# ScalarE in written order through sixteen attention pairs, with the next tile's split, the late exp and the shared values product at new places

## The chip, the cores and the metric

The kernel runs on one core of a Trainium2 chip. The metric is the device time of one execution in microseconds (us), as a median of several. The engines are TensorE (PE, matmuls), VectorE (DVE), ScalarE (ACT), GpSimd (POOL) and SyncE (SP), which issues most DMAs. Each engine runs its own instructions in order; between engines semaphores make an instruction wait for another's result.

## What is computed

```python
scores = cap * np.tanh(scale * np.matmul(q, k.transpose(0, 1, 3, 2)) / cap)   # 4 x 12 heads, 448 x 64
attn = np.exp(scores - max); attn /= attn.sum(-1) + 1e-9
x = np.matmul(attn, v)                     # -> 1792 tokens x 768
h = x @ w_in                               # 768 -> 1024
solu = h * softmax(h)
ln = (solu - mean) / np.sqrt(var + 1e-6) * g_ln
x = ln @ w_out                             # 1024 -> 768
logits = x @ w_gate + modality_bias[modality_id]
e_idx = np.argmax(logits, axis=1)          # one of 8 experts for each token
out[mask] = gate_w * (np.maximum(x[mask] @ w1[e], 0) @ w2[e])
```

## The kernel before

Three stages share one program. **Attention** goes over 24 pairs (b, p): batch b of 4, two heads of 64 in a pair p of 6. The first eight pairs are *plain*, in the code's word, and run while weights are loaded and split (0 to 94 us). The sixteen *late* pairs (n = 8 to 23, that is (1,2) to (3,5)) run from 94 to some 368 us, interleaved with the first **SoLU tiles** t of 128 tokens (14 in all; the rest runs until 460 us). Then come routing and **eight experts** (460 to 728 us).

A late pair has 448 keys: three chunks of 128 and 64 left over. The left-over keys of an even p and of p + 1 share one tile: chunk "h", whose scores, tanh and exp (e_h) are made in the second half of the even pair, and whose product with the values, q, is made for both pairs at once by `a_quarters`. Names in rows carry b, p and chunk: sc1_5_0 are the scores of pair (1,5), chunk 0; e their tanh and then exp; es sums of e; av the product of e with the values; X the attention result of a batch; kh, kl, qh, ql the high and low parts of k and q, cast by ACT or DVE (for q of pairs 11, 15 and 23, that is (1,5), (2,3) and (3,5), by ACT). rt and rb (three for a batch) bring the reciprocal sums of the batch before, by which X is multiplied.

A tile of the SoLU part has these steps: `m_split` splits X into xh and xl, `m_h` multiplies (h, 36 matmuls of 512 columns, three products of high and low parts), `m_act` takes the row maximum, exp (u), h times u and the statistics of the LayerNorm, `m_tr` transposes u on PE (lt) and splits it into lh and ll, `m_y` multiplies by w_out (y, two halves), and `m_out` scales y (ys), takes one small exp for the router (junk) and stores it. lg are the router's logits, computed by DVE from y, and read by junk.

`unit(n, cp)` writes one half of a pair: scores and tanh (`a_scp`), exp (`a_exp`), some SoLU steps (`fill`), products with the values (`a_av`), parts of the finish of the batch before (`finish`), sums (`a_esp`), and the split of the next pair (`a_split`). SoLU steps wait in the list `msteps`; `fill` takes as many as a rate allows, and `settle` takes more where the written clock says that no PSUM tile is free.

The order in which an engine runs is that of the code where a `manual_schedule` names the engine, and is otherwise chosen by the framework's scheduler. Through the late pairs only PE is named: ACT, DVE, POOL and SP are placed by the scheduler. PSUM holds three large tiles "A" (128 x 2 x 512) that go round among sc, h, lt, y, q, sum, rt and rb, in the order in which the program asks for them. So the first matmul into one waits until the last reader of its previous content, on ACT or DVE, is done.

Of the kernel before, what the change touches and what calls it, by code (L numbers as in the profile page):

```python
# [41 lines left out]
EARLY = 10  # L42
# [37 lines left out]
XCD = (1, 2, 3, 4, 5, 7, 9, 10, 12, 13, 14, 15, 16, 17, 18, 19, 20)  # L80
VACT = 0
OGA = 5
W = (0.6, 0.8, 0.45)
FW = (1, 0.7, 1.3)

# [2 lines left out]
def attn_moe_kernel(ctx, tc, kq, vv, vl, w_in, w_out, packed, ids, mbias, w1, w2, out):  # L88
# [543 lines left out]
    def m_act(t):  # L632
        s = st[t]
        h = s.pop("h")
        clock.leave(f"h{t}", 4.6)
        clock.ready[t] = clock.t + 7.2
        clock.work(1.1)
        u = mp.tile([P, 2, 512], F32, tag="m4", name=f"u{t}", bufs=4)
        sm = mp.tile([P, 8], F32, tag="sm", name=f"sm{t}", bufs=4)
        s["sm"] = sm  # L640
        dve.tensor_reduce(sm[:, 0:1], h, axis=AX.XY, op=ALU.max, negate=True)
        act.activation(u, h, AF.Exp, bias=sm[:, 0:1], accum_out=sm[:, 1:2])
        dve.tensor_mul(u, u, h)
        bn = mp.tile([P, 2, 6], F32, tag="bn", name=f"bn{t}")
        for i in range(2):
            dve.bn_stats(bn[:, i, :], u[:, i, :])
        dve.bn_aggr(sm[:, 2:4], bn)
        dve.tensor_scalar(u, u, sm[:, 2:3], None, op0=ALU.subtract)
        s["u"] = u
        (dve if t in SMD else pool).tensor_scalar(sm[:, 1:2], sm[:, 1:2], 1e-9, None, op0=ALU.add)  # L650
        dve.reciprocal(sm[:, 4:5], sm[:, 1:2])
        pool.tensor_tensor(out=sm[:, 5:6], in0=sm[:, 4:5], in1=sm[:, 4:5], op=ALU.mult)
        pool.tensor_tensor(out=sm[:, 5:6], in0=sm[:, 5:6], in1=sm[:, 3:4], op=ALU.mult)
        pool.tensor_scalar(sm[:, 5:6], sm[:, 5:6], 1e-6, None, op0=ALU.add)
        pool.tensor_tensor(out=sm[:, 6:7], in0=sm[:, 5:6], in1=mhalf, op=ALU.pow)
        pool.tensor_tensor(out=sm[:, 7:8], in0=sm[:, 6:7], in1=sm[:, 4:5], op=ALU.mult)
# [167 lines left out]
    def a_av(b, p, chunks=range(4)):  # L824

        if 0 in chunks:
            avt[b, p] = btile(f"av{b}_{p}")
            if p == 0:
                spt[b] = psS.tile([P, 512], F32, tag="S", name=f"S{b}")
        o, v = avt[b, p], vt[b, p]  # L830
        end = 3 if plain(b, p) else 2
        clock.spend(0.75 * len(chunks), "columns")
        if direct(b, p) or p % 2 and end in chunks:
            clock.spend(0.75, "strips")
        for c in chunks:
            for j in range(2):
                pe.matmul(o[64 * j:64 * j + 64, :S], v[:, c, 64 * j:64 * j + 64], et[b, p, c][:, j, :],  # L837
                          start=(c == 0), stop=(c == end))
        if direct(b, p):
            for c in chunks:  # L840
                for j in range(2):
                    g = 2 * j + c % 2
                    pe.matmul(spt[b][32 * g:32 * g + 32, :S], zone[:CK, 31 - p:63 - p], et[b, p, c][:, j, :],
                              start=(p == 0 and c < 2), stop=(p == NP - 1 and c > 1))
        elif p % 2 and end in chunks:
            for j in range(2):
                for i in range(2):
                    g, pp = 2 * j + i, p - 1 + i
                    pe.matmul(spt[b][32 * g:32 * g + 32, :S], zone[:, 31 - pp:63 - pp], est[b, pp][:, j, :],
                              start=(p == 1), stop=(p == NP - 1))  # L850
        if end in chunks:
            x = xtile(b)[:, p, :]
            if convs and b + p:
                later["x"].append(lambda: dve.tensor_copy(x, o[:, :S]))
            elif plain(b, p):
                (dve.tensor_copy if b * NP + p in XCD else act.copy)(x, o[:, :S])
            else:
                dve.tensor_add(x, x, o[:, :S])
            if p == NP - 1:
                a_ssb(b)  # L860

    def a_quarters(b, p):
        settle()
        t = atile(f"q{b}_{p}")
        for g in range(2):
            r = slice(64 * g, 64 * g + 64)
            for j in range(2):
                c = slice(64 * j, 64 * j + 64)
                pe.matmul(t[c, g, :S], vt[b, p][r, 3, c], et[b, p, "h"][r, j, :], start=True, stop=True)
        clock.spend(0.75, "quarters")  # L870
        clock.work(1.0)
        clock.leave(f"q{b}_{p}", clock.act - clock.t + 0.1)
        act.copy(xtile(b)[:, p:p + 2, :], t[:, :, :S])

    sums = {}

# [46 lines left out]
    msteps, drained = [], set()  # L923

    def push_tile(t):
        msteps.append((0.0, lambda: m_split(t), 0))
        hs = [(W[0], lambda hf=hf, d=d: m_h(t, hf, d), hf == 0 and d == 0) for hf in range(2) for d in range(ND)]
        if t and t - 1 not in drained:
            hs.insert(ND + (TRP[t - NTILE + 3] if t > NTILE - 4 else 0), (W[1], lambda: m_tr(t - 1), 1, t - 1))
        msteps.extend(hs)  # L930
        msteps.append((0.0, lambda: m_act(t), 0))
        final = t == NTILE - 1
        if final:
            msteps.append((0.0, lambda: e_first(), 0))
        if t and t - 1 not in drained:
            push_y(t - 1, t if final and TRO else None)
        if final:
            if not TRO:
                msteps.append((0.9, lambda: m_tr(t), 1))
            n = len(msteps)  # L940
            push_y(t)
            msteps.insert(n + ETD, (0.0, lambda: e_tr(), 1))
# [13 lines left out]

    def pick():

        if len(msteps[0]) > 3 and clock.t < clock.ready.get(msteps[0][3], 0.0):
            return int(all(x[0] == W[0] and not x[2] for x in msteps[1:4]))  # L960
        return 0

# [38 lines left out]
    def unit(n, cp):  # L1001
        nonlocal mp
        b, p = pairs[n]
        early = plain(b, p) and b > 0
        strips, trs = later["strip"], later["pe"]
        later["strip"], later["pe"] = [], []

        def run(fs):
            while fs:
                fs.pop(0)()  # L1010

        late_ = not plain(b, p)
        if late_ and not cp:
            m = pairs[n - 1]
            if plain(*m):
                a_av(*m, chunks=(2, 3))
            else:
                if not m[1] % 2:
                    a_quarters(*m)
                a_av(*m, chunks=(2,))  # L1020
        a_scp(b, p, cp)
        if n == 1 and not cp:
            a_av(*pairs[0], chunks=(2, 3))
        flush("cast")
        if early and p:
            flush("gate")
            if not cp:
                finish(b - 1, 4)
            else:
                run(strips)  # L1030
                flush("gate")
                cv.release()
                mp = tc.alloc_tile_pool(name="mp", bufs=2, reuse_waits="tile")
                do_step()
        a_exp(b, p, cp)
        if early and cp and not p:
            flush("gate", "sub")
            finish(b - 1, 2)
        if late_:
            pass  # L1040
        elif cp == 0 and n > 1:
            a_av(*pairs[n - 1], chunks=(2, 3))
        elif cp:
            a_av(b, p, chunks=(0, 1))
        if convs:
            convs.pop(0)()
        flush("gate", "x")
        run(strips)
        flush("gate")
        if early and p and not cp:  # L1050
            finish(b - 1, 5)
        run(trs)
        if early and cp and not p:
            flush("gate")
            finish(b - 1, 3)
        fill(FW[0])
        if late_ and cp:
            a_av(b, p, chunks=(0, 1))
        if b > 0 and not plain(b, p):
            finish(b - 1, 4 * p + 2 * cp)  # L1060
        flush("sub")
        if n == 1 and cp:
            setup_third(*tables)
        a_esp(b, p, cp)
        if n + 1 < len(pairs):
            a_split(*pairs[n + 1], cp)
        fill(FW[1])
        if cp == 1 and n + 2 < len(pairs):
            a_load(*pairs[n + 2])
        if cp == 0 and n + 1 < len(pairs):  # L1070
            v_load(*pairs[n + 1])
        fill(FW[2])
        if b > 0 and not plain(b, p):
            finish(b - 1, 4 * p + 2 * cp + 1)
        while early and p and sums_:
            conv_og(sums_[0], atile(f"po{sums_.pop()}")[:, 0, :NE])
# [3 lines left out]
    with tc.manual_schedule(engines={ET.PE, ET.Activation, ET.DVE, ET.SP}):  # L1080
# [17 lines left out]
        for n in range(FIXED):  # L1098
            unit(n, 0)
            unit(n, 1)  # L1100
    with tc.manual_schedule(engines={ET.PE}):
        for n in range(FIXED, len(pairs)):
            unit(n, 0)
            unit(n, 1)
# [697 lines left out]
```

## Time and profile before

| | us |
|---|---|
| median of 3 runs (730.03 to 731.84) | 731.14 |
| the profiled execution | 729.99 |
| its span, first to last instruction | 728.3 |
| PE busy | 711.6 (98% of the span) |
| DVE busy | 433.4 (60%) |
| ACT busy | 372.3 (51%) |
| POOL busy | 112.6 (15%) |

The profiled execution is 1.7 us longer than its span. The chain of work that ended last is to 87% on PE, to 4% each on DVE and ACT. Busy time of PE comes from modelled ends of pipelined matmuls, so neighbouring rows overlap a little. A row of the timeline gives start, duration, engine, line, operation, output <- input, partitions x elements, how many instructions it groups, and in brackets the engine's idle time ahead of it and what ended it.

### The profile page before, as it was taken

The page shows a single profiled execution, that of the slowest core. Times are in us where ns is not written, and L with a number is a line of the kernel's source. Part 1 is how long each engine was busy: PE and PEld are TensorE (multiplying, and loading weights), DVE is VectorE, ACT ScalarE, POOL GpSimd, SP SyncE. Part 2 cuts the span into 40 slices and gives each one's busy share as a digit, 9 for nine tenths or more (in the row PEclk, how much of TensorE's full clock was granted, in tenths as well). Part 3 has the DMA queues.
Part 4 walks back from the last instruction along what each step waited for, and adds up shares of the span by engine and source line. Part 5 has one row for each costly group of instructions (what it writes and reads, how often), then busy time and mean ns, then how long its engine had stood idle before and what let it go on. Part 6 is the DMA issues. An engine that isn't in the chain of part 4 may idle for free.

```text
span 728.3 us, 11174 instructions
## 1 busy us (share of the span) xinstructions
PE 711.6 (98%) x4294; PEld 544.2 (75%) x4294; DVE 433.4 (60%) x726; ACT 372.3 (51%) x506; POOL 112.6 (15%) x208
## 2 busy tenths in 40 slices
PE   8999999999999999999999999999999999999996
PEld 3344456475667666677698999998879998799995
DVE  7999656666656648455466546965256173473632
ACT  7999666665556554555521225354154162553522
POOL 5000111311012021121041211114010220002011
PEclk9999999999999999999999999999999999999998
DMA  7776120211111120200003101579928359574550
GB/s 253 262 269 241 41 76 12 88 62 38 61 41 60 46 75 13 84 15 34 22 23 124 44 30 59 172 283 320 408 76 279 120 173 402 236 238 152 210 167 26
DMA packets 29569, 97.14 MB, mean 133 GB/s; under 512 B 4087, under 2 KB 6149, under 8 KB 28738
## 3 DMA queue, kind: packets, MB, share of 16 engines
q1 hardware_dynamic: 25794, 79.47, 30.7%
q0 software_dynamic: 3568, 16.83, 6.4%
q8 instruction: 36, 0.59, 0.3%
q14 instruction: 27, 0.22, 0.1%
q10 hardware_dynamic: 144, 0.03, 0.1%
HBM read 85.24 MB, written 11.27 MB: 133 GB/s over the span
## 4 chain that ended last, share of the span: by engine, by line
PE 87%; DVE 4%; ACT 4%; DMA 2%; issue 2%; POOLq 1%; POOL 0%; SPq 0%; another core or an unknown queue 0%; DVEq 0%
PE av L837 7%; PE sc L790 7%; PE y L683 6%; PE h L627 6%; PE y L686 5%; PE y L684 5%; PE h L630 5%; PE h L628 5%; PE poD L1506 3%; PE poD L1508 3%; PE poD L1507 3%; PE phD L1400 3%; PE phD L1402 3%; PE phD L1401 3%; DMA rawc<-in_w_out_dram 2%
## 5 line engine op out<-in xcount | busy, mean ns | idle before, releaser
L797 ACT ACTIVATE e<-sc,sc 128x896 f32<-128x896 f32 (+1 forms) x80 | 78.6, 1004 | 58.6 <-PE sc L790 58.4
L803 ACT ACTIVATE e<-e,pk 128x896 f32<-128x896 f32 (+1 forms) x80 | 81.8, 1045 | 1.3
L683 PE MATMUL y<-wouh,lh 128*128 128x392 f32 (+1 forms) x224 | 78.8, 352 | 1.1 <-ACT e L797 1.1
L684 PE MATMUL y<-woul,lh 128*128 128x392 f32 (+1 forms) x224 | 75.8, 339 | 0.0
L837 PE MATMUL av<-e,v 128*64 128x448 f32 (+1 forms) x320 | 70.9, 555 | 0.7 <-ACT e L803 0.7
L686 PE MATMUL y<-wouh,ll 128*128 128x392 f32 (+1 forms) x224 | 71.3, 339 | 0.0
L627 PE MATMUL h<-winh,xh 128*128 128x512 f32 x168 | 69.6, 414 | 0.4 <-ACT xh L610 0.4
L628 PE MATMUL h<-winl,xh 128*128 128x512 f32 x168 | 66.0, 393 | 0.0
L630 PE MATMUL h<-winh,xl 128*128 128x512 f32 x168 | 61.2, 391 | 0.0
L683 PEld LDWEIGHTS y<-wouh,lh 128*128 128x128 f32 x224 | 42.0, 188 | 12.9 <-issue 10.3
L837 PEld LDWEIGHTS av<-e,v 128*64 128x64 f32 (+1 forms) x320 | 18.6, 135 | 39.3 <-issue 25.9
L1344 DVE TENSOR_TENSOR wl_D<-raw_D,wh_D 128x768 fp32r<-128x768 f32 (+1 forms) x28 | 29.9, 1071 | 27.0 <-ACT wh_D L1343 26.7
L627 PEld LDWEIGHTS h<-winh,xh 128*128 128x128 f32 x168 | 31.5, 188 | 18.0 <-issue 11.2
L1344 DVE TENSOR_TENSOR wl_H<-raw_H,wh_H 128x768 fp32r<-128x768 f32 (+1 forms) x28 | 29.2, 1069 | 23.2 <-ACT wh_H L1343 23.2
L1506 PE MATMUL poD<-wh_D,hhD 128*128 128x384 f32 x128 | 43.0, 336 | 0.0
L1507 PE MATMUL poD<-wl_D,hhD 128*128 128x384 f32 x128 | 42.8, 334 | 0.0
L1508 PE MATMUL poD<-wh_D,hlD 128*128 128x384 f32 x128 | 42.8, 334 | 0.0
L684 PEld LDWEIGHTS y<-woul,lh 128*128 128x128 f32 x224 | 42.1, 188 | 0.5
L686 PEld LDWEIGHTS y<-wouh,ll 128*128 128x128 f32 x224 | 41.9, 188 | 0.0
L1343 ACT CAST wh_D<-raw_D 128x768 fp32r<-128x768 f32 (+1 forms) x28 | 26.0, 933 | 29.8 <-DMA raw_D<-in_w_dram 29.5
L744 POOL TENSOR_TENSOR kl<-kqr,kh 128x448 fp32r<-128x448 f32 x16 | 20.2, 1261 | 132.5 <-ACT kh L743 66.7
L1400 PE MATMUL phD<-xh_D,wh_D 128*128 128x512 f32 x96 | 37.5, 390 | 1.3 <-DVE e_ob L1208 1.3
(409 smaller groups left out, 1594.6 us busy)
## 6 DMA issues: line engine op xcount, KB each, us to landing
kqr<-in_kq_dram SPq DMA_DIRECT2D x20, 448.0 KB, 4.5
rawc<-in_w_out_dram SPq DMA_DIRECT2D x8, 768.0 KB, 5.0
rawc<-in_w_in_dram SPq DMA_DIRECT2D x6, 1024.0 KB, 4.7
raw_D<-in_w_dram SPq DMA_DIRECT2D x12, 512.0 KB, 5.0
wr_T<-in_w_dram SPq DMA_DIRECT2D x16, 384.0 KB, 6.0
raw_D<-in_w_dram SPq DMA_DIRECT2D x16, 384.0 KB, 4.7
wr_T<-in_w_dram SPq DMA_DIRECT2D x12, 512.0 KB, 9.0
raw_H<-in_w_dram SPq DMA_DIRECT2D x12, 512.0 KB, 7.7
```

The source lines that it names most:

```text
L627: pe.matmul(o, s["xh"][d], winh[d][:, c], start=(d == 0), stop=False)
L628: pe.matmul(o, s["xh"][d], winl[d][:, c], start=False, stop=False)
L630: pe.matmul(o, s["xl"][i], winh[i][:, c], start=False, stop=(i == ND - 1))
L683: pe.matmul(o, s["lh"][f], wouh[f][:, c], start=(f == 0), stop=False)
L684: pe.matmul(o, s["lh"][f], woul[f][:, c], start=False, stop=False)
L686: pe.matmul(o, s["ll"][i], wouh[i][:, c], start=False, stop=(i == NF - 1))
L797: act.activation(e, t[:m, :, :S], AF.Tanh, scale=sc8[:m])
L803: act.activation(e, e, AF.Exp, scale=cap_t[:m])
L837: pe.matmul(o[64 * j:64 * j + 64, :S], v[:, c, 64 * j:64 * j + 64], et[b, p, c][:, j, :], start=(c == 0), stop=(c == end))
L1506: pe.matmul(p, hh[:, f, o], wh[:, c], start=(f == 0), stop=False)
L1507: pe.matmul(p, hh[:, f, o], wl[:, c], start=False, stop=False)
L1508: pe.matmul(p, hl[:, f, o], wh[:, c], start=False, stop=(f == NF - 1))
```

## The change

- Through the late pairs ACT, like PE, runs in written order.
- `m_act` keeps the row maximum; exp and the rest go into `m_exp`, written two list entries later (UDEL = 2) or ahead of the next late unit's scores. For late tiles (t >= EARLY) both stay together.
- `m_split(t)` is put into the list behind `m_exp(t - 1)` instead of at its end.
- `a_quarters` of an even pair moves from the start of the odd pair's first half to behind that half's first `fill`, so q comes after the odd pair's first two score tiles.
- X of an even late pair is made by an ACT copy of av, q's first half is added by DVE, and its second half is copied by ACT. Before, ACT copied all of q and DVE added av.

```diff
 def m_act(t):
         dve.tensor_reduce(sm[:, 0:1], h, axis=AX.XY, op=ALU.max, negate=True)
+        s["uh"] = u, h
+
+    def m_exp(t):
+        s = st[t]
+        if "uh" not in s:
+            return
+        u, h = s.pop("uh")
+        sm = s["sm"]
         act.activation(u, h, AF.Exp, bias=sm[:, 0:1], accum_out=sm[:, 1:2])
...
+            elif p % 2:
+                dve.tensor_add(x, x, o[:, :S])
             else:
-                dve.tensor_add(x, x, o[:, :S])
+                act.copy(x, o[:, :S])
...
         clock.spend(0.75, "quarters")
-        clock.work(1.0)
-        clock.leave(f"q{b}_{p}", clock.act - clock.t + 0.1)
-        act.copy(xtile(b)[:, p:p + 2, :], t[:, :, :S])
+        x = xtile(b)
+        dve.tensor_add(x[:, p, :], x[:, p, :], t[:, 0, :S])
+        act.copy(x[:, p + 1, :], t[:, 1, :S])
...
     def push_tile(t):
-        msteps.append((0.0, lambda: m_split(t), 0))
+        at = [i for i, x in enumerate(msteps) if x[3:] == ("act", t - 1)]
+        msteps.insert(len(msteps) if t >= EARLY else at[0] + 1 if at else 0, (0.0, lambda: m_split(t), 0))
...
+        if t >= EARLY:
+            act_ = msteps[n - 1 - final][1]
+            msteps[n - 1 - final] = (0.0, lambda: (act_(), m_exp(t)), 0)
+        else:
+            msteps.insert(min(n + UDEL, len(msteps)), (0.0, lambda: m_exp(t), 0, "act", t))
...
-            if plain(*m):
-                a_av(*m, chunks=(2, 3))
-            else:
-                if not m[1] % 2:
-                    a_quarters(*m)
-                a_av(*m, chunks=(2,))
+            a_av(*m, chunks=(2, 3) if plain(*m) else (2,))
+        if late_:
+            for t in list(st):
+                m_exp(t)
         a_scp(b, p, cp)
...
         if late_ and cp:
             a_av(b, p, chunks=(0, 1))
+        elif late_ and p % 2:
+            a_quarters(b, p - 1)
...
-    with tc.manual_schedule(engines={ET.PE}):
+    with tc.manual_schedule(engines={ET.PE, ET.Activation}):
```

How it moves instructions, at three places. First ACT between the pairs (1,3) and (1,5), where the cast qh1_5 stands. Before, it lies between the last tanh and the last exp of pair (1,3):

```order
L672 CAST lh0_1090<-lt0_1081 128x512
L743 CAST kh1_5_1165<-kqr1_5_1122 128x448
L797 ACTIVATE e1_3_2_1103<-sc1_3_2_1096,sc8_67 128x896
L743 CAST qh1_5_1241<-kqr1_5_1122 128x448
L672 CAST lh0_1090<-lt0_1081 128x512
L803 ACTIVATE e1_3_2_1103<-e1_3_2_1103,pk_62 128x896
```

After, it follows both exps of the second half of pair (1,4), one of them that of e_h:

```order
L806 ACTIVATE e1_4_2_1237<-sc1_4_2_1225,sc8_67 128x896
L806 ACTIVATE e1_4_h_1238<-sc1_4_h_1232,sc8_67 128x896
L812 ACTIVATE e1_4_2_1237<-e1_4_2_1237,pk_62 128x896
L812 ACTIVATE e1_4_h_1238<-e1_4_h_1238,pk_62 128x896
L752 CAST qh1_5_1250<-kqr1_5_1123 128x448
L869 COPY X1_807<-av1_4_1243 128x448
L806 ACTIVATE e1_5_0_1276<-sc1_5_0_1262,sc8_67 128x896
```

The cast has moved behind the tiles of a whole pair, and tanh and exp now come in twos.

Second, ACT in the first half of pair (2,1), before (ys1 and junk1 belong to SoLU tile 1, xh3 to tile 3):

```order
L873 COPY X2_1539<-q2_0_1534 128x896
L797 ACTIVATE e2_1_0_1558<-sc2_1_0_1544,sc8_67 128x896
L803 ACTIVATE e2_1_0_1558<-e2_1_0_1558,pk_62 128x896
L797 ACTIVATE e2_1_1_1559<-sc2_1_1_1551,sc8_67 128x896
L803 ACTIVATE e2_1_1_1559<-e2_1_1_1559,pk_62 128x896
L610 CAST xh3_0_1624<-X1_807 128x3x64
L797 ACTIVATE e2_1_2_1607<-sc2_1_2_1600,sc8_67 128x896
L697 ACTIVATE ys1_1595<-y1_1449,sm1_1170 128x776
L803 ACTIVATE e2_1_2_1607<-e2_1_2_1607,pk_62 128x896
L699 ACTIVATE junk1_1597,ys1_1595<-lg_75 128x8
L743 CAST qh2_3_1795<-kqr2_3_1641 128x448
L610 CAST xh3_1_1630<-X1_807 128x3x64
```

and after:

```order
L806 ACTIVATE e2_1_0_1554<-sc2_1_0_1540,sc8_67 128x896
L806 ACTIVATE e2_1_1_1555<-sc2_1_1_1547,sc8_67 128x896
L812 ACTIVATE e2_1_0_1554<-e2_1_0_1554,pk_62 128x896
L812 ACTIVATE e2_1_1_1555<-e2_1_1_1555,pk_62 128x896
L884 COPY X2_1538<-q2_0_1560 128x448
L706 ACTIVATE ys1_1598<-y1_1437,sm1_1171 128x776
L708 ACTIVATE junk1_1600,ys1_1598<-lg_75 128x8
L806 ACTIVATE e2_1_2_1610<-sc2_1_2_1603,sc8_67 128x896
L812 ACTIVATE e2_1_2_1610<-e2_1_2_1610,pk_62 128x896
L611 CAST xh3_0_1627<-tail0_789 128x3x64
L611 CAST xh3_0_1627<-X1_807 128x3x64
```

xh3_0 stood ahead of the third tanh and stands now behind ys1, junk1, the third tanh and its exp. On DVE the steps that these rows wait for stand, after the change, in this order:

```order
L916 TENSOR_TENSOR rh_72<-rt1_1529,rh_72 12x448
L883 TENSOR_TENSOR X2_1538<-X2_1538,q2_0_1560 128x448
L928 TENSOR_TENSOR X1_807<-X1_807,rb1_0_1570 128x896
L822 TENSOR_TENSOR es2_1_1574<-e2_1_0_1554,e2_1_1_1555 128x896
L928 TENSOR_TENSOR X1_807<-X1_807,rb1_1_1589 128x896
L829 TENSOR_TENSOR es2_1_1574<-es2_1_1574,e2_0_h_1481 64x896
L697 SCALAR_TENSOR_TENSOR lg_75<-y1_1437,sm1_1171,bias_t_73 128x8
L752 CAST kh2_3_1707<-kqr2_3_1644 128x448
L699 TENSOR_REDUCE lg_75<-lg_75 128x1
L928 TENSOR_TENSOR X1_807<-X1_807,rb1_2_1618 128x896
L825 TENSOR_TENSOR es2_1_1574<-es2_1_1574,e2_1_2_1610 128x896
```

lg1, which junk1 reads and for which ys1 waits by its semaphore, comes behind two products X times rb1 and two sums.

Third, PE in pair (3,1). Before, q3_0 stands ahead of the scores, and the transposes lt5 and products h6 lie between scores and rb2_0:

```order
L903 MATMUL rt2_2386<-ident_61,rr2_2358 44x112 x4
L869 MATMUL q3_0_2393<-e3_0_h_2318,v3_0_2146 64x448 x4
L837 MATMUL av3_0_2347<-e3_0_2_2317,v3_0_2146 64x448 x2
L790 MATMUL sc3_1_0_2403<-qh3_1_2364,kh3_1_2276 128x448 x2
L790 MATMUL sc3_1_0_2403<-ql3_1_2365,kh3_1_2276 128x448 x2
L790 MATMUL sc3_1_0_2403<-qh3_1_2364,kl3_1_2277 128x448 x2
L790 MATMUL sc3_1_1_2410<-qh3_1_2364,kh3_1_2276 128x448 x2
L790 MATMUL sc3_1_1_2410<-ql3_1_2365,kh3_1_2276 128x448 x2
L790 MATMUL sc3_1_1_2410<-qh3_1_2364,kl3_1_2277 128x448 x2
L663 MATMUL lt5_2423<-ident_61,u5_2208 128x128 x8
L627 MATMUL h6_2344<-winh0_115,xh6_0_2336 128x512
```

After, q3_0, rb2_0, rb2_1 and the third score tile follow one another:

```order
L628 MATMUL h6_2349<-winh5_120,xh6_1_2239 128x512
L629 MATMUL h6_2349<-winl5_126,xh6_1_2239 128x512
L631 MATMUL h6_2349<-winh5_120,xl6_1_2240 128x512
L880 MATMUL q3_0_2455<-e3_0_h_2331,v3_0_2151 64x448 x4
L921 MATMUL rb2_0_2462<-rh_72,sel_71 128x448 x2
L921 MATMUL rb2_1_2480<-rh_72,sel_71 128x448 x2
L799 MATMUL sc3_1_2_2499<-qh3_1_2369,kh3_1_2289 128x448 x2
L799 MATMUL sc3_1_2_2499<-ql3_1_2370,kh3_1_2289 128x448 x2
L799 MATMUL sc3_1_2_2499<-qh3_1_2369,kl3_1_2290 128x448 x2
L692 MATMUL y5_2509<-wouh0_127,lh5_2411 128x392
```

The products h6 that stood between now stand ahead of the scores.

## Rows read from the trace of the kernel before

**Rows 1.** Table of stretches (busy us of each engine, PEclk, DMA share, GB/s)

```profile
94.00:368.00 274.00, 268.50 (x1507) 181.21 (x1506) 164.92 (x254) 155.35 (x200) 43.18 (x71) 1.00 0.14 48
368.00:460.00 92.00, 91.96 (x519) 84.44 (x519) 56.82 (x137) 27.94 (x48) 21.15 (x82) 1.00 0.19 66
```

**Rows 2.** Waits of PE's queue, 94 to 368 us: us, times, longest

```profile
PE q L869 <- ACT e_h L803: 2.0, 3, 0.8
PE y L683 <- ACT e L797: 1.1, 1, 1.1
PE lt L663 <- ACT e L797: 1.0, 2, 0.5
```

**Rows 3.** Timeline of ACT, pair (1,4): start, us, engine, line, operation

```profile
127.37 1.01 ACT L797 ACTIVATE e<-sc,sc 128x896 f32<-128x896 f32 x1 [2.38 <-PE sc L790]
128.41 1.04 ACT L803 ACTIVATE e<-e,pk 128x896 f32<-128x896 f32 x1
129.36 0.99 ACT L797 ACTIVATE e_h<-sc_h,sc 128x896 f32<-128x896 f32 x1
130.38 1.04 ACT L803 ACTIVATE e_h<-e_h,pk 128x896 f32<-128x896 f32 x1
```

**Rows 4.** Timeline of ACT, a copy of 448 columns

```profile
146.08 0.53 ACT L879 COPY ssb<-S 128x448 f32<-128x448 f32 x1 [4.19 <-PE S L849]
```

**Rows 5.** Timeline of PE, pair (1,4), q

```profile
131.47 0.98 PE L869 MATMUL q<-e_h,v 64*64 64x448 f32 x8 [0.84 <-ACT e_h L803]
```

**Rows 6.** Timeline of DVE, pair (1,4)

```profile
131.46 1.08 DVE L820 TENSOR_TENSOR es<-es,e_h 64x896 f32<-64x896 f32 x1 [0.88 <-ACT e_h L803]
...
133.18 1.45 DVE L744 TENSOR_TENSOR ql<-kqr,qh 128x448 fp32r<-128x448 f32 x1
```

**Rows 7.** Timeline of DVE, pair (2,1)

```profile
171.65 1.09 DVE L917 TENSOR_TENSOR X<-X,rb 128x896 f32<-128x896 f32 x1 [0.89 <-PE rb L910]
...
178.18 0.61 DVE L744 TENSOR_TENSOR ql<-kqr,qh 128x448 fp32r<-128x448 f32 x1
```

**Rows 8.** Timeline of PE, pair (2,1)

```profile
165.16 0.98 PE L869 MATMUL q<-e_h,v 64*64 64x448 f32 x8
...
175.04 0.40 PE L627 MATMUL h<-winh,xh 128*128 128x512 f32 x1
...
177.19 0.50 PE L627 MATMUL h<-winh,xh 128*128 128x512 f32 x1 [0.36 <-ACT xh L610]
...
179.91 0.97 PE L837 MATMUL av<-e,v 128*64 128x448 f32 x4
```

**Rows 9.** Timeline of PE, pair (1,3)

```profile
107.10 0.47 PE L790 MATMUL sc<-qh,kh 64*128 64x448 f32 x2
...
110.25 1.07 PE L663 MATMUL lt<-ident,u 128*128 128x128 f32 x8 [0.30 <-DVE u L648]
```

**Rows 10.** Timeline of ACT, pair (1,3)

```profile
108.02 1.01 ACT L797 ACTIVATE e<-sc,sc 128x896 f32<-128x896 f32 x1 [1.81 <-PE sc L790]
```

**Rows 11.** Timeline of ACT, pair (2,1)

```profile
172.77 0.35 ACT L610 CAST xh<-X 128x192 fp32r<-128x192 f32 x1 [0.81 <-DVE X L917]
...
173.96 0.91 ACT L697 ACTIVATE ys<-y,sm 128x776 f32<-128x776 f32 x1
...
175.70 0.29 ACT L699 ACTIVATE junk<-lg 128x8 f32<-128x8 f32 x1
```

**Rows 12.** Timeline of PE, pair (3,1)

```profile
273.62 1.09 PE L663 MATMUL lt<-ident,u 128*128 128x128 f32 x8 [0.48 <-ACT e L797]
...
282.00 0.45 PE L683 MATMUL y<-wouh,lh 128*128 128x392 f32 x1 [1.10 <-ACT e L797]
```

**Rows 13.** Table of stretches behind the last matmul

```profile
722.00:722.50 0.50, 0.18 (x1) 0.00 (x0) 0.00 (x0) 0.00 (x0) 0.00 (x0) 1.00 0.07 16
...
724.50:725.00 0.50, 0.00 (x0) 0.00 (x0) 0.00 (x0) 0.00 (x0) 0.50 (x1) 0.56 0.00 0
```

**Rows 14.** Timeline of PE, the start

```profile
1.45 3.20 PE L1089 MATMUL warm<-rh 128*128 128x448 f32 x8 [1.45 <-DVE rh L132]
```

More of the change, by code (lines that the diff above doesn't have):

```diff
@@ L82 @@
 OGA = 5
+UDEL = 2
 W = (0.6, 0.8, 0.45)
@@ L932, in push_tile @@
         final = t == NTILE - 1
+        n = len(msteps) + final
         if final:
@@ L957, in pick @@
     def pick():
-        if len(msteps[0]) > 3 and clock.t < clock.ready.get(msteps[0][3], 0.0):
+        if len(msteps[0]) == 4 and clock.t < clock.ready.get(msteps[0][3], 0.0):
             return int(all(x[0] == W[0] and not x[2] for x in msteps[1:4]))
```

## Prediction

> **What bounds the kernel now.** I read the table of stretches first: from 94 to 368 us TensorE (PE) is busy 268.50 of 274 us, from 368 to 460 91.96 of 92 [rows 1]. ScalarE (ACT) is busy 155.35 of those 274, VectorE (DVE) 164.92. So the kernel is bound by PE, and the stretch of the late pairs holds 5.5 us in which PE does nothing. That is the most that a new order of ACT can give back. What it can cost has no such bound: a wait of PE there ends later, and the 92 us behind have no slack to take it up.
>
> The list of waits of PE's queue in that stretch names where the 5.5 us lie: the shared values product q for the exp of e_h (2.0 in three places), the first half of y for a tanh (1.1), the transposes lt for a tanh (1.0 in two places) [rows 2]. All are of one kind: PE wants something that ACT (or DVE behind it) has not delivered, or a PSUM tile whose last reader is on ACT. So the question is place by place whether ACT and DVE, in the new order, deliver earlier or later.
>
> **What the change does to ACT's spacing.** Before, the two halves of a pair's scores go tanh, exp, tanh, exp at 127.37, 128.41, 129.36, 130.38 [rows 3]: 1.04 from a tanh to its own exp, 0.95 to an independent one. After, tanh, tanh, exp, exp: three steps of 0.95, the first exp 0.9 later, the last 0.15 earlier. The second score tile is released about 1 us earlier. What comes behind the exps in program order now really stands behind them.
>
> **The sum, by places of TensorE.** Work on PE is nearly the same; q is only moved. A copy of 128x896 (0.91) becomes two of 128x448 on ACT, 0.53 each by the copy of the same shape [rows 4], and one DVE add stays one. These are off PE's path where ACT has slack.
>
> (1) *Pairs (1,4)/(1,5), (2,2)/(2,3), (3,4)/(3,5).* q1_4 waits until e_h's exp is done: it starts at 131.47 after 0.84 idle [rows 5]; the second place is the same and the third 0.33, which makes the 2.0 [rows 2]. Rows that follow each other undelayed overlap by some 0.08, so 0.92, 0.92 and 0.41 go when q moves out, and PE is free at 130.55. But the next pair's scores then come at once, and their qh is cast on ACT behind the two exps, where it lay two tiles earlier. By that spacing: tanh 127.37 and 128.32, exp 129.27 and 130.22, done 131.26; the cast (0.56 for 448 columns) is done at 131.75. ql on DVE follows the sum of e_h, which starts at 131.46 and takes 1.08 [rows 6], so it starts at about 132.45. ql takes 0.61 [rows 7] or 1.45 [rows 6]; I take the short one, as for the one other ql whose qh ACT casts. It is there at 133.06, where PE, without the wait for q, would want it at 130.55 + 0.90 (av, 0.97 less the overlap [rows 8]) + 0.31 (the two matmuls with qh) = 131.76: a stall of 1.30 in place of 0.92. Net +0.4 in each place, the third too (0.8 for 0.41), **+1.1**; with the long ql +3.6, with both hidden -2.3.
>
> (2) *Pair (1,3), transposes lt0.* The three PSUM tiles A go round; now lt0 gets the tile that q1_2 had, whose last reader is ACT's second copy. That copy stands behind tanh, tanh, exp, exp: scores' start + 0.92 until the tanh starts (107.10 to 108.02 [rows 9, 10]) + 4 x 0.95 + 0.53 = +5.25. PE has 4.04 of work between (scores 1.42, three h 0.72, q 0.92, third score tile 0.71, changes of form). Stall 1.2 where 0.3 idle, 0.48 with the overlap of three h, was [rows 9]; 0.2 more for h1 behind it: **+0.95**. If ACT ran freely: -0.5.
>
> (3) *Pair (2,1), the largest.* Before, PE runs q at 165.16, h3 at 175.04, a stall inside h3 at 177.19, av's last chunk at 179.91 [rows 8]. The cast xh3_0 ran at 172.77, ahead of the third tanh [rows 11]. After, in program order: both exps, copy of q2_0, ys1, junk1, tanh and exp of the third tile, and only then xh3_0. Worked forward from the rows: scores at 166.06 (q no longer ahead), tanh 166.98 to 167.99, and q, whose tile it must leave, waits 0.5 behind scores that end at 167.48; last exp done at 170.87, the copy of q at 171.3, and rb1_1, which waits for this copy's tile, 0.3 late, so the third score tile goes at 172.4 and PE, with av (1.65) and rb1_2 behind it, stands at h3 at 175.4. ys1 waits for lg1 on DVE, and lg1 stands in DVE's order behind X times rb1_0, a sum, X times rb1_1 and a sum, four of 1.09 [rows 7] from 170.1, so lg1 is there at 174.6. Then ys1 until 175.6 [rows 11], junk1 (0.3), tanh from 175.9, exp from 176.93, xh3_0's two casts of 0.35 [rows 11], done at 178.5. PE waits 3.1 us there. Its xl parts come in time behind it. With 0.5 and 0.3, less the 0.53 that the stall inside h3 cost, and less what q's tile and rb saved before: av's last chunk at 182.85 where 179.91 was, **+2.95**. Bounds: if lg1 were at once there, ys1 follows the copy at 171.3 and the third tanh is bound by its scores, h3 goes at about 176.3: +0.8. If DVE slips a further operation, +4.0.
>
> (4) *Pair (3,1).* Before: lt5 waits 0.48 at 273.62, y5 1.10 for tanh at 282.00 [rows 12]. After, q and av change places with h6, and rb2_0, rb2_1 and the third score tile follow q with no filling between. rt until 269.8, av 0.9, lt5 0.85 and fifteen h of 0.23: scores at 275.1; tanh 276.02, exps until 279.9, copy of q3_0 done at 280.4; rb2_1, which needs that tile, stood ready at 278.75, behind scores 1.4, three h 0.8, q 0.95 and rb 0.45 (stall 1.65). The third score tile needs the tile of rb2_0, which DVE multiplies after the sum es: 279.95 + 2 x 1.09 = 282.1 (stall 1.4). y5 needs the tanh of it: 282.1 + 0.92 + 1.01 = 284.1, where 282.00 stood: **+2.1**. If copy and sum came before: +0.
>
> (5) *Pair (3,3):* y6 stands so that it waits for the tanh of the pair's first tile, 1.95 behind the scores' start with 1.42 of work between: **+0.55**, at least 0. (6) Three more changes of the row form of q and a tile of (2,5): **+0.25**.
>
> The other halves I find even. u's exp, two steps later, costs nothing: its readers, lt, stand a whole tile of y behind, some 5 us; without that cover it would cost its 1.1 each time.
>
> Sum 1.1 + 0.95 + 2.95 + 2.1 + 0.55 + 0.25 = **+7.9 us**. The profiled execution took 729.99, so 737.9; the median of the runs shown lies 1.15 above it, so 739.0. I take 738.5.
>
> **Rivals.**
> *A, the forecast:* places 1 to 4 all cost, 735.7 to 742. 0.47.
> *B, the other side, faster.* The waits for q, lt0 and lt5 go (0.92 + 0.92 + 0.41 + 0.48 + 0.48 = 3.2), and the new ones are hidden since casts and copies meet a less loaded ACT (57% busy [rows 1]). It decides at the point where qh, ql, xh3_0 and the copy of q3_0 together cost PE under 3.2 - 2.2 = 1.0 us more than nothing. 731.14 - 3.2 = 728, and 5.5 is the whole reserve. Against it: xh3_0 alone stands behind seven ACT operations, one bound to DVE. 0.08.
> *C, only the two large ones.* Places 1 and 2 break even as DVE takes the sums earlier, and 3 and 4 cost 1.5 to 3 less than I work out: 733.5 to 735.7. For it: scores and sums move with ACT, and each stall gives ACT and DVE time to catch up. 0.24.
> *D, the clock.* PE's clock is granted at 1.00 throughout the stretch [rows 1]. Behind the last matmuls, which end at 722.18, it is at 0.56 in 724.5 to 725, the lower level (1.2 for 2.4 GHz) within that slice [rows 13]; PE had done nothing between. A stall of 3.1 us at h3 would be by far the longest pause of PE in the stretch, where the longest now is 1.1 [rows 2]. The eight warm matmuls at the start took 3.20 us, 0.40 each of 448 columns [rows 14], where av's four of that size take 0.97 [rows 8]; one such stretch at the lower level costs half, 1.6 us, at h3 and perhaps at rb2_1: 740.5 to 742.5. 0.11. The Trainium skill, "TensorE: Matmul & The Clock Gate", section "HAM oscillation — how this bites in real kernels", says that idle gaps between bursts of matmuls let the gate close, so that the next burst begins cold. By that rule D happens; the fall behind the last matmul agrees with it, but no gap between two matmuls of this trace does it.
> *E, nothing changes by over 0.3%:* some 0.3% (2.2 us) is what a measurement of this kernel can tell from no change. PE's queue re-sorts the stalls and the net is under 2.2: 729 to 733.3. 0.10.
>
> **Range.** A, C and D make slower 0.82, E 0.10, B 0.08. Below, I reach into E, to 731.8; above, D and the long ql (738.5 + 2.5 + 1.6 = 742.6) and a DVE slip at h3 go to 743.5. That leaves out about 0.13 below and 0.06 above.
>
> **What would show it.** After: waits of PE of over 2 us at h3 for xh3_0 (pair (2,1)), 1 to 2 us at rb2_1 and the third score tile of (3,1), about 1 us at lt0 and at the ql matmul of the scores of (1,5), (2,3), (3,5); no wait of q for e_h; PE busy unchanged at 711 to 712 while the span grows; and the stretch behind 368 just as long, only later. I am wrong if lg1 comes before 173 (then place 3 falls to +0.8), if ql is cast while PE is still at work, or if DVE does X times rb2_0 before the sum. The largest single mistake would be place 3.

## The result and the profile after

The changed kernel takes **741.33 us** (median of 4, 740.81 to 742.5) beside 731.49 for the kernel before in the same runs: ratio 1.0129, interval 1.0089 to 1.0169. It is 9.8 us slower; 738.5 was forecast, with 731.8 to 743.5 as the range. The profiled execution is the slowest of the four, 742.5 us with a span of 740.8; that of before, with 729.99, is among the fastest of its kernel, so the two traces lie 12.5 us apart, some 2.7 more than the medians. One of the four executions of the kernel before took 735.19; its later series, of 9 to 17 executions, have medians of 730.66 to 731.34.

Where PE's queue waits, 94 to 379 us of the changed kernel (us in total, times, longest), in answer to [rows 2]:

```profile
PE h L628 <- ACT xh L611: 3.1, 1, 3.1
PE sc L799 <- DVE ql L753: 2.7, 3, 1.0
PE y L692 <- ACT e L806: 1.6, 2, 1.1
PE rb L921 <- ACT X L884: 1.3, 1, 1.3
PE sc L799 <- DVE X L928: 1.1, 1, 1.1
PE lt L672 <- ACT X L884: 1.1, 1, 1.1
```

No q waits for e_h any more. In its place stand the waits that the prediction named: h3 for xh3_0, three scores for ql, rb2_1 for the copy of q, the third score tile for X times rb, lt0 for the copy of q.

One sign did not come: PE's busy time was to stay at 711 to 712 us and is 719.3. From 95.2 to 381.7 us, which is 94 to 368 in the trace of before, PE idles 12.2 us instead of 5.5 and is busy 274.3 instead of 268.5; a lower clock, shown below, is part of that. The stretch behind is 359.1 us for 360.3.

Place (1), pair (1,5), PE and DVE, in answer to [rows 5] and [rows 6]:

```profile
134.00 0.47 PE L799 MATMUL sc<-qh,kh 64*128 64x448 f32 x2 [0.18 <-ACT qh L752]
135.46 0.47 PE L799 MATMUL sc<-ql,kh 64*128 64x448 f32 x2 [0.99 <-DVE ql L753]
...
134.79 0.61 DVE L753 TENSOR_TENSOR ql<-kqr,qh 128x448 fp32r<-128x448 f32 x1
```

Place (3), pair (2,1). ACT, in answer to [rows 11]:

```profile
173.41 0.52 ACT L884 COPY X<-q 128x448 f32<-128x448 f32 x1
177.49 0.91 ACT L706 ACTIVATE ys<-y,sm 128x776 f32<-128x776 f32 x1 [3.57 <-issue]
178.44 0.30 ACT L708 ACTIVATE junk<-lg 128x8 f32<-128x8 f32 x1
...
178.74 0.99 ACT L806 ACTIVATE e<-sc,sc 128x896 f32<-128x896 f32 x1
179.76 1.04 ACT L812 ACTIVATE e<-e,pk 128x896 f32<-128x896 f32 x1
180.71 0.33 ACT L611 CAST xh<-tail 128x192 fp32r<-128x192 f32 x1
180.95 0.35 ACT L611 CAST xh<-X 128x192 fp32r<-128x192 f32 x1
```

and DVE in the same stretch:

```profile
174.95 1.08 DVE L928 TENSOR_TENSOR X<-X,rb 128x896 f32<-128x896 f32 x1
176.06 1.09 DVE L829 TENSOR_TENSOR es<-es,e_h 64x896 f32<-64x896 f32 x1
177.18 0.23 DVE L697 SCALAR_TENSOR_TENSOR lg<-y,sm,bias_t 128x8 f32<-128x8 f32 x1
```

ACT stands still for 3.57 us ahead of ys1, until DVE has lg1 at 177.41. The profile names no releaser for this wait ("<-issue"); that it is lg1 is inferred: here, and in the traces of e3, e6, e7 and e8 (next section), ys1 starts 0.08 to 0.09 us behind lg1's end. The tanh behind it, whose scores were long there, and the cast xh3_0 behind that, wait with it. PE, in answer to [rows 8]:

```profile
181.34 0.79 PE L628 MATMUL h<-winh,xh 128*128 128x512 f32 x1 [3.12 <-ACT xh L611]
...
182.36 0.63 PE L628 MATMUL h<-winh,xh 128*128 128x512 f32 x1
182.79 0.63 PE L629 MATMUL h<-winl,xh 128*128 128x512 f32 x1
...
187.26 0.39 PE L629 MATMUL h<-winl,xh 128*128 128x512 f32 x1
187.49 0.84 PE L631 MATMUL h<-winh,xl 128*128 128x512 f32 x3
```

Behind the 3.12 us in which it had nothing to do, its matmuls start 0.43 apart instead of 0.23, thirteen of them, and then 0.23 again. The table of stretches shows why (PEclk stands behind the five engines' busy times):

```profile
180.00:181.00 1.00, 0.00 (x0) 0.00 (x0) 0.17 (x1) 1.00 (x3) 0.00 (x0) 0.57 0.71 286
181.00:182.00 1.00, 0.66 (x2) 0.56 (x3) 1.00 (x2) 0.80 (x4) 0.00 (x0) 0.50 0.28 112
...
187.00:188.00 1.00, 1.00 (x6) 0.75 (x4) 0.00 (x0) 0.00 (x0) 0.00 (x0) 1.00 0.00 0
```

The clock was at its lower level from 180 to 187 us, which costs 13 x 0.20 = 2.6 us. That is rival D, which had put 1.6 on it.

Place (4), pair (3,1), PE, in answer to [rows 12]:

```profile
289.51 0.68 PE L921 MATMUL rb<-rh,sel 128*128 128x448 f32 x2 [1.26 <-ACT X L884]
...
291.30 0.47 PE L799 MATMUL sc<-qh,kh 64*128 64x448 f32 x2 [1.12 <-DVE X L928]
...
293.26 0.69 PE L692 MATMUL y<-wouh,lh 128*128 128x392 f32 x1 [1.10 <-ACT e L806]
293.76 0.53 PE L693 MATMUL y<-woul,lh 128*128 128x392 f32 x1
294.08 0.53 PE L692 MATMUL y<-wouh,lh 128*128 128x392 f32 x1
294.41 0.53 PE L693 MATMUL y<-woul,lh 128*128 128x392 f32 x1
```

Three waits in a row, as worked out; and y5's matmuls then start 0.33 apart instead of 0.18, nine of them: some 1.3 us, again the clock (0.50 from 293 to 296).

**All places in one table.** I took the start of one named group of matmuls in each trace (for instance the third score tile of (1,5)) less its start in the trace of before. The table has by how much this grows from one group to the next, in us, so each column is one place. "Start" is the difference at the third score tile of (1,2): it is from the first stage, whose code the change leaves alone. The sum is without it. The runs are those of the next section.

| run | start | (1,3) | (1,5) | (2,1) | (2,3) | (2,5) | (3,1) | (3,3) | (3,5) | sum |
|---|---|---|---|---|---|---|---|---|---|---|
| changed | 1.21 | +1.07 | +0.57 | +5.50 | +0.58 | +0.22 | +3.45 | +0.53 | +0.57 | +12.5 |
| changed, again | 3.62 | +1.07 | +0.57 | +5.58 | +0.62 | +0.22 | +3.45 | +0.54 | +0.56 | +12.6 |
| e1_pe_only | 0.34 | +0.95 | -0.94 | +0.43 | -0.91 | +0.23 | +4.98 | +1.42 | -0.40 | +5.8 |
| e3_q_old | 2.85 | -0.40 | -0.22 | +1.97 | -0.22 | 0 | -0.46 | 0 | -0.21 | +0.5 |
| e4_act_only | 2.36 | -0.41 | -0.22 | +1.96 | -0.23 | +5.95 | +2.74 | +4.26 | +4.22 | +24.6 |
| e8_act_split | -0.31 | -0.40 | -0.22 | +3.59 | -0.20 | 0 | +2.69 | 0 | -0.20 | +5.3 |
| e2_h3_busy | 1.48 | +1.08 | +0.56 | +3.00 | +0.60 | +0.22 | +3.56 | +0.54 | +0.58 | +10.1 |
| e5_qh_dve | 1.27 | +1.08 | -0.95 | +4.52 | -0.92 | +0.22 | +4.31 | +0.55 | -0.40 | +8.4 |
| e7_xh3_dve | 0.80 | +1.08 | +0.58 | +0.08 | +0.58 | +0.22 | +4.93 | +0.54 | +0.59 | +8.6 |
| e6_q_three | 1.77 | -0.41 | +0.58 | +3.58 | +0.59 | 0 | -0.46 | 0 | +0.60 | +4.5 |
| v1_before_q3 | 2.36 | 0 | -0.94 | 0 | -0.92 | 0 | 0 | 0 | -0.39 | -2.3 |
| v4_act_q3 | 1.58 | -0.39 | -0.95 | +0.61 | -0.92 | 0 | -0.46 | 0 | -0.38 | -2.5 |
| v2_pe_q3 | 1.61 | 0 | -0.95 | 0 | -0.92 | 0 | 0 | 0 | -0.39 | -2.3 |

(e4 has +6.28 more in (2,0), where no other run differs.) All later work is PE-bound, but it moves the end of a trace by -1.7 to +0.7 us beside start and sum; most of that is one wait of PE in the experts (phD for DVE, 1.3 us), which is there in the traces of before, e3, e5, e6, v1, v2 and v4 and in none of the others.

The medians, each less that of the kernel before in its own series, agree with the sums to 1.8 us, except for the changed kernel: +9.8 and +10.3 for +12.5 and +12.6. So the table says where the time goes in one traced execution; how much of it an execution has on average, only the median says.

### The profile page after: what moved, and what is told of

The parts are those of the page before. It is cut to its first block, busy times and chain, and to the rows that moved or that the text cites. A ratio compares the mean times of both kernels' runs of the same rounds, so it can differ in the third digit from the quotient of the medians.

```text
span 740.8 us, 11167 instructions
## 1 busy us (share of the span) xinstructions
PE 719.3 (97%) x4294; PEld 547.5 (74%) x4294; DVE 432.9 (58%) x726; ACT 369.5 (50%) x514; POOL 112.9 (15%) x208
## 4 chain that ended last, share of the span: by engine, by line
PE 89%; ACT 4%; issue 2%; DVE 2%; DMA 1%; POOLq 1%; POOL 0%; another core or an unknown queue 0%; DVEq 0%
PE av L846 8%; PE sc L799 8%; PE h L628 6%; PE y L692 6%; PE h L629 5%; PE h L631 5%; PE y L695 5%; PE y L693 5%; PE poD L1524 3%; PE poD L1526 3%; PE poD L1525 3%; PE phD L1420 3%; PE phD L1418 3%; PE phD L1419 3%; PE S L852 2%
## 5 line engine op out<-in xcount | busy, mean ns | idle before, releaser
L812 ACT ACTIVATE e<-e,pk 128x896 f32<-128x896 f32 (+1 forms) x80 | 79.8, 1042 | 0.3
L628 PEld LDWEIGHTS h<-winh,xh 128*128 128x128 f32 x168 | 32.3, 192 | 22.1 <-issue 12.2
L1419 PE MATMUL phD<-xl_D,wh_D 128*128 128x512 f32 x96 | 37.4, 389 | 0.0
```

The source lines that it names most:

```text
L628: pe.matmul(o, s["xh"][d], winh[d][:, c], start=(d == 0), stop=False)
L812: act.activation(e, e, AF.Exp, scale=cap_t[:m])
```

## The experiments

**ACT's order taken back alone.**

```diff
-    with tc.manual_schedule(engines={ET.PE, ET.Activation}):
+    with tc.manual_schedule(engines={ET.PE}):
```

> The changed kernel, but ACT is again placed by the scheduler through the late pairs (engines: PE alone); q, exp and split stay at their new places. Theory (ACT's written order makes xh3_0, qh and with it ql late): no wait of PE at h3 of pair (2,1) over 0.8 us, no wait of the scores of (1,5), (2,3), (3,5) for ql, clock 1.00 from 164 to 190 us; the waits of pair (3,1) at rb2_1 and the third score tile stay, since q3_0 still follows the scores, 2 to 3 us with the clock. Median 731 to 735. Rival (the new place of q and the tiles that follow it are what costs): the waits at h3 and at (1,5) stay and the median is 738 or more.

Measured 735.78, ratio 1.0073 (1.006 to 1.0086), just above what the theory gave. As it said, no wait at h3 over 0.2 us, no ql late, the three places of q gain 0.94, 0.91 and 0.40. But (3,1) costs 4.98, where 2 to 3 were expected, and (1,3) 0.95 without ACT's order. Its waits:

```profile
PE y L692 <- ACT e L806: 2.5, 2, 1.4
PE rb L921 <- ACT X L884: 1.9, 1, 1.9
```

So these two places are q's: the copy of q stands behind two tanh and two exp whatever orders ACT (in (3,1) of this run behind u's exp, 1.09 us, as well). The clock is 0.91 on average from 260 to 300 us here, which is part of the 4.98.

**ACT's order alone, on the kernel before.** The same line the other way, and nothing else.

> The kernel before with ACT in written order through the late pairs and nothing else of the change. Theory: xh3_0 stands behind ys1, junk1 and the third tanh and exp, so h3 of (2,1) waits 2 to 3.5 us and the clock falls behind it (some 2.5 us more); pair (3,1) and the transposes lt0 cost nothing new; q still waits 2 us in three places. Median 735 to 738. Rival (q's place): within 1 us of the kernel before, 730.5 to 732.5.

Measured 754.07, ratio 1.0308 (1.0292 to 1.0325): both theories missed, by 16 us and more. Its waits:

```profile
PE h L627 <- ACT xh L610: 14.6, 5, 3.8
PE y L683 <- DVE X L917: 2.7, 1, 2.7
```

I had counted the late xh once, at h3. In the kernel before, `m_split` stands at the end of the list of steps, so with ACT in written order the casts of five tiles come just when PE wants them, and the granted clock of the traced execution falls to 0.982. It did not fall behind each of these waits:

```profile
164.00:190.00 26.00, 22.78 (x134) 15.03 (x134) 17.73 (x28) 13.58 (x21) 4.98 (x9) 1.00 0.18 62
...
185.59 0.50 PE L627 MATMUL h<-winh,xh 128*128 128x512 f32 x1 [3.00 <-ACT xh L610]
...
317.40 0.80 PE L627 MATMUL h<-winh,xh 128*128 128x512 f32 x1 [2.54 <-ACT xh L610]
```

Behind 3.00 us at h3 it held at 1.00; behind 2.54 us at 317.40 it was at 0.50 until 320, with the matmuls 0.43 apart.

**q back at its old place, ACT in written order.** `a_quarters` again ahead of av's last chunk, q copied whole by ACT and av added by DVE.

> The changed kernel with the shared values product q at its old place and copied whole by ACT, as before; ACT in written order, exp and split of the SoLU tile at their new places. Theory: the costs of (3,1) (3.5 us), of lt0 (1.1 us) and of ql in three places go, the wait at h3 of (2,1) with its clock (5 us) stays: median 735.5 to 738. Rival (everything hangs on ACT's order): 740 or more. Second rival (everything hangs on q): 732 or less.

Measured 732.41, ratio 1.0026 (1.0016 to 1.0036): less than the theory gave, and near the second rival. The wait of 3.0 us at h3 is there, but the clock holds behind it:

```profile
164.00:190.00 26.00, 22.51 (x134) 15.13 (x133) 14.26 (x22) 12.61 (x19) 2.91 (x3) 1.00 0.13 42
```

(2,1) then costs 1.97, and five other places gain 0.2 to 0.5 each (q waits 1.3 us in all instead of 2.0, for instance). ACT's written order, with exp and split as the change has them, costs 0.5 us over the stretch of this trace and 1.8 by the medians; most of the change's cost needs q at its new place. Executions of this kernel differ in the clock: the mean granted clock of the twelve is 0.994 to 0.997, and the four at 0.997 took 731.39 to 731.9, the others 731.76 to 734.45.

**The early split alone, with ACT's order.** e4 with `m_split` right behind row maximum and exp of the tile before, close to the change's place (there exp stands two list entries later); exp stays behind the row maximum.

```diff
-        msteps.append((0.0, lambda: m_split(t), 0))
+        at = [i for i, x in enumerate(msteps) if x[3:] == ("act", t - 1)]
+        msteps.insert(len(msteps) if t >= EARLY else at[0] + 1 if at else 0, (0.0, lambda: m_split(t), 0))
```

> The kernel before with ACT in written order, and of the change beside it only the place of the split (behind the row maximum and exp of the tile before, instead of at the list's end). Exp of the SoLU tile stays right behind the row maximum, q at its old place. Theory: what makes ACT's written order alone so dear (754 us) is the cast xh at the end of the list, so that PE waits for it at h in five places; with the split early only h3's wait of 3 us is left, as in the changed kernel with q at its old place: median 731.5 to 734. Rival (the exp that stands right behind the row maximum blocks ACT's tanh): 736 or more.

Measured 735.18, ratio 1.0059 (1.0045 to 1.0072): 19 us better than e4, so the split's place was that cost, but above the expected range. Two things are left over e3: at (2,1) the clock fell (0.93 in 164 to 190, +3.59 for +1.97), and y5 in (3,1) waits 2.7 us for DVE:

```profile
PE h L627 <- ACT xh L610: 3.0, 1, 3.0
PE y L683 <- DVE X L917: 2.7, 1, 2.7
```

The later exp is what takes the second away in e3.

**PE kept at work ahead of h3.**

```diff
             s["h"] = atile(f"h{t}")
+            for _ in range(BUSY if t == 3 else 0):
+                pe.matmul(s["h"][:, 0, :], winh[0][:, :P], winh[1][:, :512], start=True, stop=True)
```

> The changed kernel with 13 more matmuls of 512 columns in front of h3 of SoLU tile 3, written into h3's own PSUM tile, which h3 then overwrites; they want only weights that are there, so they run while PE waits for xh3_0. They add work and take nothing else away. Theory (the clock falls since PE stands still for 3 us): clock 1.00 from 181 to 187 us, the matmuls of h3 0.23 apart instead of 0.43, 2.0 to 2.6 us less, median 738.7 to 739.5. Rival (h3 is slow for another reason, or the added matmuls come in its way): median 741 or more.

The added 13 fill PE's wait; h3 starts 0.25 us behind the end of the cast xh3_0 (181.59), as they end a little late. Its matmuls start 0.23 apart, and (2,1) falls from 5.50 to 3.00. The 13, h3's first matmul, and the clock in the two stretches:

```profile
178.74 3.26 PE L628 MATMUL h<-winh,winh 128*128 128x512 f32 x13 [0.21 <-ACT ys L709]
181.84 0.39 PE L631 MATMUL h<-winh,xh 128*128 128x512 f32 x1
...
164.00:190.00 26.00, 25.05 (x140) 16.68 (x140) 14.85 (x23) 11.42 (x19) 3.17 (x4) 1.00 0.17 56
260.00:300.00 40.00, 36.53 (x199) 26.47 (x198) 25.27 (x41) 19.39 (x26) 8.04 (x14) 0.96 0.13 42
```

So in the trace the 2.5 us are the clock's. That they hang on PE standing still, one trace does not show by itself, since e3 and e4 hold the clock behind the same pause; but none of the seven traces without a pause of 3 us at h3 has a fall there, and five of the seven with one do. The time, 740.3 (ratio 1.0131, 1.0116 to 1.0146), lies between the two expectations. Beside its own series of the kernel before it is 9.6 us slower, and the changed kernel 9.8 and 10.3: in the times the gain is not clear of noise, and where it went stays open.

**qh cast by DVE; xh3 cast by DVE.** Two kernels, each with one entry of a table less.

```diff
-QHA = (8, 11, 15, 23)
+QHA = (8,)
```

```diff
-XHA = (0, 2, 3, 5, 7, 9, 11, 12)
+XHA = (0, 2, 5, 7, 9, 11, 12)
```

> The changed kernel, with the high parts of q of pairs (1,5), (2,3) and (3,5) cast by DVE instead of ACT. Theory: their qh and ql then come before the sums of the pair ahead, PE does not wait for ql or qh at the scores of these pairs, and what moving q saves is left: each place goes from +0.57 to between 0 and -0.9. The rest stays as it was. Median 737.3 to 739.5. Rival (the scores wait for something else there): 741 or more.

> The changed kernel, with X split into xh for SoLU tile 3 by DVE instead of ACT. Theory (xh3_0 is late only because it stands behind ys1, junk1, the third tanh and its exp on ACT): no wait of PE at h3 over 0.8 us, clock 1.00 from 164 to 190 us, the step of +5.5 us in pair (2,1) falls to +0.3 to +0.8. Median 735.5 to 737.5. Rival (DVE with its products and sums sets h3's start anyway): a wait of 2 us or more stays, 739.5 or more.

e5: 738.42, ratio 1.0095 (1.008 to 1.0109), as expected: the three places go from +0.57 to -0.95, -0.92 and -0.40. e7: 738.03, ratio 1.0087 (1.0074 to 1.01): at (2,1) all that was expected and more, +0.08 with the clock at 1.00; but behind it (3,1) grew from 3.45 to 4.93, since its three waits now meet a clock that falls for longer:

```profile
164.00:190.00 26.00, 25.05 (x142) 16.69 (x141) 15.35 (x24) 12.79 (x18) 2.92 (x3) 1.00 0.14 49
260.00:300.00 40.00, 36.53 (x187) 25.06 (x186) 22.78 (x35) 17.20 (x24) 6.54 (x11) 0.91 0.12 40
```

That is more than the 0.5 us by which it missed the range. (In e5 too, 0.91 there and +4.31; at h3 its clock was low for 4 us instead of 7, +4.52. So the rest did not stay as it was.)

**q late only where it waited.** `a_quarters` at the new place for three pairs, otherwise at the old one with its old copy (not shown).

```diff
+LATEQ = ((1, 4), (2, 2), (3, 4))
...
-        elif late_ and p % 2:
+        elif late_ and (b, p - 1) in LATEQ:
             a_quarters(b, p - 1)
```

> The changed kernel, with the shared values product at its new place only for pairs (1,4), (2,2) and (3,4), and at its old place, with its old copy, for (1,2), (2,0), (2,4), (3,0) and (3,2). ACT in written order. Theory (each place is its own cost, and they add up): (1,3), (2,5), (3,1) and (3,3) go to between -0.5 and 0, (2,1) is +2 with h3's wait but a clock at 1.00, the three q places stay at +0.57: about +2.5 in all, median 732.5 to 734.5. Rival (the places act on each other, so that late parts pile up): 737 or more.

Measured 736.25, ratio 1.0058 (1.0042 to 1.0075): above the range and below the rival. Each place did what it was to do, except that the clock fell at h3 (+3.58 for the +2 expected) behind the same wait of 3.0 us as in e3:

```profile
181.00:182.00 1.00, 1.00 (x4) 0.72 (x3) 0.16 (x1) 0.00 (x0) 0.00 (x0) 0.50 0.00 0
```

Not every execution has this fall: the six have mean clocks of 0.994 to 0.999, and the lowest time, 733.26 at 0.999, lies in the expected range; the highest is 737.61 at 0.994.

**Versions that beat both.** The kernel before with only these three q late; the same with later exp and earlier split; and e6 with both table entries of e5 and e7.

> The kernel before, with nothing but the shared values product (and its three-part copy) at the new place for pairs (1,4), (2,2) and (3,4); ACT placed by the scheduler. Theory: there qh is cast early, so the three waits for the exp of e_h go and nothing takes their place, as with PE alone in written order, where these places gained 0.94, 0.91 and 0.39: 2.2 us less than the kernel before, median 727.8 to 729.3. Rival (the gain is eaten by the mode changes of the rows, or by later tiles): 730 to 731.5.

> The kernel before with q late for the three pairs, as in the version that gained 0.35%, and besides with the later exp and the earlier split of the SoLU tile as in the change; ACT placed by the scheduler. Theory: where the scheduler places ACT, exp and split of a tile are placed by it too and their place in the code matters little: within 0.7 us of that version, 728.3 to 730. Rival (the later exp of u makes h's PSUM tile free later, and PE waits for it): 731 or more.

> The changed kernel with the three repairs that the runs point to, together: the shared values product late only for pairs (1,4), (2,2) and (3,4), the high parts of q of (1,5), (2,3), (3,5) cast by DVE, and X split into xh for SoLU tile 3 by DVE. ACT in written order. Theory (the costs are apart, and add up): the three q places gain 0.94, 0.92 and 0.39, (1,3) and (3,1) gain 0.4 each, (2,1) is between -1 and 0, no wait of PE at h3, clock 1.00 throughout: 2.7 to 4 us less than the kernel before, median 727.0 to 728.6. Rival (what DVE takes over delays its sums and products elsewhere): 729.5 or more.

v1: 729.22, ratio 0.9965 (0.9954 to 0.9977). v2: 729.3, 0.9972 (0.996 to 0.9983). v4: 729.1, 0.9966 (0.9952 to 0.9979), 0.5 above its range. All three gain 2.3 to 2.5 us in the stretch and some 2 in the median. Where the scheduler places ACT, the place of exp and split in the code indeed makes no difference beyond the noise (v1 and v2). In v4 DVE now sets h3 ("<- DVE xl", 0.9), which takes back most of what (1,3) and (3,1) gain. In v1's waits q is gone, and nothing has come in its place:

```profile
PE y L684 <- ACT e L798: 1.1, 1, 1.1
PE lt L664 <- ACT e L798: 1.0, 2, 0.5
PE rb L918 <- ACT e L798: 0.4, 2, 0.3
```

**The changed kernel again.**

> The changed kernel once more, unaltered, for a second trace and more times, since the clock behind a pause of 3 us at h3 fell in some traces and not in another. If the fall belongs to this order of work, the step of pair (2,1) is +5.5 us again and the mean clock from 164 to 190 us 0.87; if it differs between executions of one kernel, the step lies anywhere from +3.0 (clock 1.00) to +5.5, and the places without a change of clock, (1,3), (1,5), (2,3), (2,5), (3,3), (3,5), are the same to 0.1 us. Median 740 to 742.

Measured 741.67, ratio 1.0149 (1.0128 to 1.0171), mean clock 0.87 again and every place within 0.08 us of the first trace. Both traces of this kernel have the fall at h3. The mean granted clock of whole executions, 0.990 to 0.993 in nine of the changed kernel and 0.997 to 0.999 in those of before, says that all nine lose to the clock: 0.006 of 740 is 4.4 us, an estimate. It does not say that the order of work alone decides it: e3, e5 and e6 differ between executions of one kernel (e5 from 736.29 us at 0.997 to 739.85 at 0.992).

## Why the prediction was right, point by point

It was right in direction and in the places, and its waits came nearly as worked out; what it had too small is the clock. By its steps:

- **Place 1**, +1.1 forecast, +1.72 measured (0.57 + 0.58 + 0.57). Mechanism right: scores wait for ql, 0.99 us at 135.46, after 0.18 for qh. ql took the short form, 0.61. The waits grew as forecast, by 1.1 (ql 2.7 and qh 0.4, where q's were 2.0), but they cost more than their idle time: without the 1.17 us of them at (1,5), in e5, the place is 1.52 us shorter. e5 shows that qh's place on ACT is the cause, and that without it the move of q gains what [rows 5] promised.
- **Place 2**, +0.95 forecast, +1.07 measured; e1 (+0.95) and e3 (-0.40) show that it is q's place, not ACT's order.
- **Place 3**, +2.95 forecast, +5.50 measured. With the clock held (e2) it is +3.00. The chain lg1, ys1, junk1, tanh, exp, xh3_0 ran as worked out; e7 shows that taking xh3 out of it takes the cost away.
- **Place 4**, +2.1 forecast, +3.45 measured, 1.3 of it the clock.
- **Places 5 and 6**, +0.55 and +0.25 forecast, +0.53 and +0.22 measured.
- **u's later exp**, costed at nothing: right. e8 shows more: with ACT in written order and the exp at its old place, y5 waits 2.7 us.

So the sum, +7.9, was too small by the clock's 3.8 us (2.5 and 1.3) and 0.6 at place 1: over the same stretch the traces have +12.5. The first stage (+1.2) and a wait in the experts that did not come (-1.3) cancel. That the time lies in the range is in part luck. The forecast's own way, 729.99 + 12.5 and the 1.15 to the median, gives 743.6, just outside 743.5; the median is 2 us lower than that, and why it is so is not shown. And the range's upper end was made with the long ql and a slip of DVE, of which neither came.

The step that I mis-weighed is **rival D**: a chance of 0.11 and a price of 1.6 us, for a fall that both traces of the changed kernel show, at h3 and at y5, and that costs 2.5 and 1.3. The rule of the Trainium skill, "TensorE: Matmul & The Clock Gate", section "HAM oscillation — how this bites in real kernels", agrees with these traces: the matmuls behind the gap begin at the lower clock. But a pause alone did not decide it. In e3, e4, e6 and e8 ACT and PE run the same order around h3, and PE waits 2.98 to 3.00 us there; the clock held in e3 and e4, at 1.00, and fell to 0.50 in e6 and e8. What decides is not shown.

What the prediction did not see is how the parts hang together. It put the cost on ACT's written order and q's move as one. The runs part them: late qh and xh3 are ACT's order (e1, e5, e7), lt0 and the waits of (3,1) are q's place (e1, e6), the early split is what keeps ACT's order from costing 23 us (e4, e8), and q's move by itself, in the three pairs where q had waited, is a gain (v1). By the medians, q and the tile's steps without ACT's order cost 5.1 us (e1), and ACT's order without q's move 1.8 (e3); together they cost 9.8 to 10.3, so some 3 us come only where the two meet, as at the late ql.

## What to carry to other kernels

Putting an engine into written order makes the code's order a schedule: first list what each cast and copy stands behind, above all behind an instruction that waits for a third engine (ys1 for lg1), since all behind it wait too. Move a product out of a wait only where its old place waits; at the five other places it only brought its copy behind later work. Where the bounding engine pauses for some us, add to the stall what its clock may lose behind it, and bring the forecast to both.

## What was new of the hardware

- Behind an idle time of 3.0 us at h3 the clock stayed at 1.00 in two kernels (e3, e4) and fell to 0.50 in two others (e6, e8) whose ACT and PE orders around it are the same; in the changed kernel, behind 3.1 us, it was low for some 7 us in both traces. In e4 it also fell behind 2.54 us. At (3,1) of the changed kernel it fell with no pause longer than 1.3 us, in the third of three waits of 1.1 to 1.3 us with little work between them.
- The first sixteen score matmuls took 3.26 us in the trace of before and 5.18 in that of the changed kernel, with the same code and a granted clock written as 1.00 in both. This is not all of the "start" column, -0.3 to +3.6 us: they took 3.26 in e3 too, which starts 2.85 late, with a clock of 0.50 from 25 to 28 us. No edit explains the column.
